# A sliding-window attention with four attention experts behind it, rewritten with other score blocks, layouts, load rules and a new list

## Chip, core, metric

The kernel runs on one core of a Trainium2 chip. The core's engines work side by side, each through its own queue in order: TensorE (PE; its weight loads are shown as PEld), VectorE (DVE), ScalarE (ACT), GpSimd (POOL) and SyncE (SP), which here only issues transfers (DMAs). Matrix products land in PSUM, which has eight banks; everything else lies in SBUF, which has 128 partitions. The metric is the device time in microseconds (us); lower is better.

## The reference, cut to what matters

Eight batches, eight heads, 576 tokens, 64 features a head. First an attention within a window of 32 tokens to both sides; its output, 512 features a token, is the input of four causal attention experts, of which each token uses two.

```python
scores = scale * np.matmul(q, k.transpose(0, 1, 3, 2))
mask = np.abs(pos[:, None] - pos[None, :]) <= 32
attn = softmax(np.where(mask, scores, -1e9))
x = np.matmul(attn, v)                  # heads side by side: [8, 576, 512]

logits = x @ w_gate                     # 4 experts
w = softmax of the 2 largest logits of a token, 0 for the others
for e in range(4):                      # one head of 64 features each
    q = x @ wq[e]; k = x @ wk[e]; v = x @ wv[e]
    a = softmax(causal(scale * (q @ k.transpose(0, 2, 1))))
    out += w[:, :, e] * (a @ v @ wo[e])
```

## The kernel before

Everything is computed in steps of a few instructions, each a small function. The string ORDER is a list of 837 steps, written out for all eight batches; the program issues them in this order, and an engine's queue holds its share of them in that order. A step's digits are its arguments (batch, head group, half, ...); what stands behind the @ names the PSUM banks. Steps of two or three batches are mixed.

*Window attention.* `lq`, `lk` load q or k of four heads (a head group) by one DMA of 576 KB: a partition gets 18 successive tokens of a head, 4608 bytes. `tq`, `tk` (both `turn`, L251) turn it on DVE, in blocks of 32 by 32, into two halves of 32 features by 576 tokens, one head on each 32 partitions; the 18 tokens of a partition are written 18 columns apart. `lv` loads V of 128 tokens at a time with eight heads side by side; `vc` (L244, L245) copies it by DMA within SBUF, so that V stands there in windows of 128 keys that start at every multiple of 64.

`sc` (L277) computes, for four heads and half of the sequence (288 queries), the scores of 64-key blocks against the queries that can see them. Blocks that start at even multiples of 64 go to PSUM partitions 0 to 63, odd ones to 64 to 127; EBLK and OBLK list them. In a block, the two feature halves of 32 are two accumulated fp32 matmuls for each of four heads, so TensorE is used as tiles of 32 rows by 64 columns. `ex` (L286) takes the exponential of two heads on ACT, `mk` (L290) multiplies by a 0/1 mask on POOL. `av` (L302) multiplies probabilities with V, 128 queries (two blocks of 64) and eight heads a step, with a 65th column of ones for the sums; step T = 4 handles the first and the last 64 queries, of which 32 each are used. `un` (L312, L313) divides by the sums on DVE and writes x with its features in an interleaved order (the feature index mod 4 outermost), to which the weight loads `lw0` to `lw2` are matched. `xt` (L322) transposes x on TensorE, `xf` (L327) copies it from PSUM in fp32 on ACT for the gate, `xb` (L337) makes a bf16 copy on POOL.

*Experts.* `ga` computes the gate's logits, `gt`, `ge`, `gm`, `gu` the two weights. `pp` and `pe` project and copy q and k of two experts, `pv` and `ve` the values, `ps` (L430) and `xe` (L436) compute causal scores and exponentials in four chunks, `se` cuts the diagonal blocks on POOL, `po` (L458) multiplies with the values, `oe` (L466) scales by gate and sum, `pt` and `ot` transpose, `py` (L482) applies the output weights, `ye` (L490) copies, `st` stores.

*Loads* are plain DMAs on SP's queue: each is issued as soon as SP is there and its buffer is free.

Of the kernel before, what the change touches and what calls it, by code (L numbers as in the profile page):

```python
# [8 lines left out]
F32 = mybir.dt.float32  # L9
# [10 lines left out]
S = 576  # L20
HS = 288
SP_ = 640

ORDER = """
    lq01 s_ones s_pads s_warm s_ident tq01 lk01 tk01 sc010@02 sc011@46 lk00 s_mask ex0100@0 mk0100 lk10 lq00
    tk00 ex0110@4 tq00 sc000@40 ex0111@6 ex0001@0 ex0000@4 lv0 sc001@60 tk10 ex0010@6 ex0101@2 lq10 tq10
    ex0011@0 lq11 vc0 lw2 lk11 lw0 lw1 lq20 lv1 tq11 mk0110 mk0111 mk0001 mk0011 mk0101 sc100@02 sc101@64
    ex1001@2 ex1010@6 mk0000 mk0010 av03@2 un03@2 av02@6 mk1010 un02@6 ex1000@0 ex1011@4 av01@0 un01@0 tk11
    lk20 av04@4 xt01@6 av00@0 xf01@6 mk1000 xb01 sc111@26 un04@4 un00@0 ex1110@2 xt02@4 cw1 xf02@4 xt00@0
    xf00@0 xb00 xb02 cw2 sc110@24 ex1101@4 ex1111@6 ex1100@2 mk1011 mk1111 lq21 ga0@0 cw0 pp001@4 gt0@0  # L30
    pp010@2 mk1100 mk1101 tq20 pe001@4 gm0 pp000@0 pp011@4 pe011@4 pv01@6 pe000@0 ge0 pe010@2 ps003@0
    ps002@2 xe003@0 mk1110 ps013@4 xe013@4 se013 ve01@6 ps000@0 vc1 mk1001 tk20 pv00@6 xe000@0 xe002@2 lk21
    ps001@0 xe001@0 ve00@6 gu0 tq21 sc200@24 ex2001@4 ex2000@2 sc201@06 av13@4 ex2011@6 ex2010@0 un13@4 lk31
    ps012@6 ps011@2 ps010@0 tk21 av14@4 un14@4 xe012@6 xe010@0 av12@6 un12@6 xe011@2 av10@0 un10@0 av11@4
    xt11@6 xf11@6 un11@4 xt12@2 se002 se003 mk2001 mk2010 po00@0 xf12@2 oe00@0 xb11 xt10@4 xb12 xf10@4
    sc211@26 sc210@40 ex2111@6 ex2110@2 ex2101@0 xb10 pp110@6 pe110@6 ex2100@4 lk30 lq30 tq30 tk30 pt00@0
    mk2011 pp111@2 pp101@6 tk31 pp100@4 pe111@2 pe101@6 lv2 lw3 cw3 pv11@1 ot00@0 ve11@1 mk2110 mk2101 se012
    mk2111 mk2100 mk2000 lq31 tq31 pe100@4 lk40 ps112@6 ps101@4 ps113@2 xe112@6 xe113@2 vc2 xe101@4 ga1@0
    sc301@26 ex3011@6 ex3010@2 gt1@0 sc300@04 tk40 mk3011 ex3001@4 ex3000@0 ps111@6 ps102@2 av22@4 un22@4
    av24@0 un24@0 xe102@2 av23@2 lq40 un23@2 av20@4 un20@4 xe111@6 mk3001 mk3010 mk3000 av21@0 sc311@26  # L40
    un21@0 tq40 sc310@04 ex3110@2 ex3111@6 ex3100@0 ex3101@4 po01@2 xt22@0 ge1 xf22@0 lk41 lq50 lq41 gm1
    oe01@2 tq41 xt21@6 xt20@4 pv10@0 ps100@2 xf20@4 xf21@6 ps103@4 mk3111 mk3101 ga2@6 ve10@0 gt2@6 lv3 lk50
    vc3 xe103@4 xe100@2 gm2 gu1 tk41 sc401@04 sc400@62 ex4010@0 mk3100 xb22 ex4001@2 ge2 ex4011@4 xb20 xb21
    pp201@0 pe201@0 pp200@2 ex4000@6 pt01@0 mk4010 ot01@0 pp210@6 pe200@2 pe210@6 ps110@0 ps200@2 xe200@2
    xe110@0 mk3110 se103 mk4001 tk50 av31@4 av34@6 un31@4 un34@6 av32@2 av33@0 un33@0 mk4000 se102 se112
    av30@6 un32@2 py00@4 py02@0 py01@2 ye02@0 ye01@2 ye00@4 pv20@0 xt31@2 tq50 un30@6 gu2 lv4 lk61 ve20@0
    st02 lq51 lk60 lk51 lq60 st01 xf31@2 sc410@46 ex4100@4 ex4101@6 se113 sc411@20 xt32@4 xf32@4 ex4111@0
    pp211@6 pe211@6 xt30@4 po11@0 mk4011 xb31 mk4101 xf30@4 mk4111 xb32 oe11@0 ex4110@2 po10@6 xb30 ps213@2
    xe213@2 ps211@4 ps210@0 ga3@2 xe210@0 xe211@4 vc4 oe10@6 gt3@2 mk4100 sc500@06 ex5000@0 ex5001@6
    sc501@42 pp301@0 tq51 tk51 ex5010@4 ex5011@2 ps203@4 xe203@4 ps202@6 xe202@6 ps212@2 ps201@4 xe212@2  # L50
    pe301@0 av41@0 un41@0 av40@6 xe201@4 un40@6 se203 mk4110 av42@2 un42@2 av44@4 av43@6 se202 mk5011 lv5
    vc5 sc510@20 ge3 ex5100@2 se212 un44@4 ex5101@0 un43@6 gm3 tk60 sc511@64 pt11@2 pv21@3 xt42@0 pt10@1
    ex5110@6 se213 mk5010 lq70 ex5111@4 ot10@1 ot11@2 pp311@6 pe311@6 ve21@3 pp300@4 tq60 gu3 pe300@4 xf42@0
    py11@6 po21@4 xt40@0 oe21@4 ye11@6 lq71 xt41@2 pp310@6 xf41@2 xf40@0 py12@4 ye12@4 pv30@2 ve30@2 pe310@6
    po20@4 oe20@4 ps311@6 ps302@0 ga4@2 xe302@0 xe311@6 gt4@2 sc601@04 ex6011@4 ex6010@0 mk5110 mk5101
    mk5111 mk5100 mk5001 xb42 sc600@62 ex6000@6 ex6001@2 av52@4 ps300@6 xe300@6 ps312@0 ps301@2 un52@4
    av53@4 xe301@2 un53@4 lv6 xb41 xb40 xe312@0 mk5000 mk6001 av50@6 av54@2 av51@0 un50@6 ps303@6 xe303@6
    un54@2 ge4 mk6000 ps313@4 ps310@2 un51@0 pp411@6 xt52@0 xe310@2 xe313@4 xt50@2 pv31@1 mk6011 xf50@2
    pe411@6 pp400@6 xt51@2 xf51@2 xf52@0 st12 lk71 lq61 tk61 ve31@1 se313 se302 pv40@4 ve40@4 se303 pe400@6
    pt20@0 pp410@2 ot20@0 tq61 po30@6 lk70 vc6 st00 lv7 pe410@2 ps413@2 xe413@2 ps412@0 ps411@4 xe412@0  # L60
    xe411@4 xb50 mk6010 py10@2 pp401@0 ye10@2 oe30@6 sc610@46 xb52 xb51 gm4 pe401@0 tk70 ex6100@4 ex6101@6
    sc611@20 ex6110@2 ex6111@0 pp501@4 pe501@4 tq70 ps403@2 se312 mk6111 mk6100 xe403@2 se403 se413 st11
    ps401@6 ps400@0 xe401@6 xe400@0 pt21@2 mk6110 mk6101 po31@4 pp500@6 pt30@3 ps402@0 oe31@4 ot30@3 ot21@2
    st10 pe500@6 xe402@0 sc701@64 tk71 sc700@02 ex7011@4 ex7010@6 ga5@4 se402 ex7001@2 ex7000@0 ps503@2
    ps410@6 xe503@2 xe410@6 gt5@4 ps501@0 ps500@2 xe501@0 xe500@2 av60@4 un60@4 av61@6 av62@0 un61@6 av63@4
    av64@6 se412 un63@4 un62@0 un64@6 py20@2 xt60@4 pv41@0 pt31@1 ve41@0 ot31@1 tq71 ye20@2 xf60@4 py22@6
    xt62@0 xf62@0 pp511@2 xt61@0 xf61@0 ye22@6 xb62 pv51@7 ve51@7 xb60 mk7010 po40@4 xb61 pe511@2 gu4 oe40@4
    pp510@0 po41@6 oe41@6 pe510@0 py21@0 ye21@0 st20 vc7 st22 st21 sc710@42 ex7100@4 ex7101@2 sc711@06 ga6@4
    mk7101 ex7111@6 ex7110@0 gt6@4 se503 mk7001 mk7100 mk7000 mk7111 ps513@6 xe513@6 ps511@2 ps502@0 xe511@2
    ps512@6 ge5 xe502@0 pp601@4 pe601@4 pp610@2 pt40@0 py30@4 pe610@2 xe512@6 py31@2 ye31@2 pt41@1 pp600@6  # L70
    pe600@6 ot40@0 pv60@2 py32@0 gm5 ot41@1 ye30@4 ye32@0 ve60@2 pv50@4 st31 ps603@2 mk7011 mk7110 se513
    ps510@0 ps601@6 xe603@2 ve50@4 av73@2 un73@2 gu5 xe510@0 av72@0 un72@0 av70@4 st32 st30 xe601@6 av74@2
    av71@6 un74@2 un71@6 un70@4 ps602@0 xe602@0 se502 po50@2 pv61@6 ve61@6 oe50@2 xt71@0 ge6 xf71@0 py42@7
    py40@4 ye40@4 xt70@0 xf70@0 ye42@7 se512 pp611@2 xt72@6 xf72@6 pe611@2 po51@4 oe51@4 ps600@2 ps612@0
    ga7@6 xe600@2 ps611@2 gt7@6 st40 xb71 xb70 se603 ps610@4 xe612@0 se602 xb72 pt51@7 py41@0 pt50@6 ot50@6
    gm7 ot51@7 xe610@4 ye41@0 xe611@2 pp701@4 pp700@0 ge7 pe700@0 py50@6 ye50@6 po60@0 gm6 pe701@4 ps703@4
    xe703@4 ps613@2 st42 st41 gu6 ps701@6 oe60@0 xe613@2 ps702@4 st50 xe702@4 ps700@2 xe700@2 xe701@6 se703
    se612 se613 pp711@0 gu7 pe711@0 py51@4 po61@2 oe61@2 py52@0 pt60@1 ye51@4 st51 pp710@6 ot60@1 ye52@0
    st52 pt61@2 pv71@3 ve71@3 ot61@2 pe710@6 ps713@6 xe713@6 ps712@0 ps711@4 xe711@4 ps710@6 xe710@6 xe712@0
    pv70@2 py61@4 py60@6 se702 se713 se712 ye61@4 ye60@6 st61 st60 ve70@2 po70@2 po71@4 oe70@2 pt70@0 oe71@4  # L80
    ot70@0 pt71@1 py62@2 ye62@2 st62 ot71@1 py71@0 ye71@0 st71 py70@2 ye70@2 st70 py72@0 ye72@0 st72
# [4 lines left out]
def kernel(  # L86
# [454 lines left out]
```

## Time and profile before

| what | us |
|---|---|
| median of 3 runs | 299.84 |
| lowest and highest run | 296.77, 302.43 |
| the profiled execution, first to last instruction (span) | 300.6 |
| PE busy with matmuls | 240.0 |
| DVE busy | 198.3 |
| ACT busy | 139.2 |
| POOL busy | 138.8 |

The profile is of one execution. Its own time is given only as the span. Busy times of engines overlap, so they don't add up; PE's ends are modelled, since its matmuls are pipelined. A fp32 matmul is recorded as two matmuls and two weight loads. "<-" behind an idle time names what ended it; "issue" stands there if nothing that the profile shows did. Lines such as L277 are lines of the kernel's file.

### The profile page before, as it was taken

The page shows a single profiled execution, that of the slowest core. Times are in us where ns is not written, and L with a number is a line of the kernel's source. Part 1 is how long each engine was busy: PE and PEld are TensorE (multiplying, and loading weights), DVE is VectorE, ACT ScalarE, POOL GpSimd, SP SyncE. Part 2 cuts the span into 40 slices and gives each one's busy share as a digit, 9 for nine tenths or more (in the row PEclk, how much of TensorE's full clock was granted, in tenths as well). Part 3 has the DMA queues.
Part 4 walks back from the last instruction along what each step waited for, and adds up shares of the span by engine and source line. Part 5 has one row for each costly group of instructions (what it writes and reads, how often), then busy time and mean ns, then how long its engine had stood idle before and what let it go on. Part 6 is the DMA issues. An engine that isn't in the chain of part 4 may idle for free.

```text
span 300.6 us, 12189 instructions
## 1 busy us (share of the span) xinstructions
PE 240.0 (80%) x5504; PEld 194.0 (65%) x5504; DVE 198.3 (66%) x351; ACT 139.2 (46%) x210; POOL 138.8 (46%) x174
## 2 busy tenths in 40 slices
PE   0745996959599589898497984999999799999973
PEld 0634974739478487777376764877777667866651
DVE  6734487866878957984819760579968527947550
ACT  1232042743356126545451454346773476278743
POOL 5358119340597245818027764053741386133210
PEclk9957598977889959999969999699999999999999
DMA  7999993199937992149957099680104413122334
GB/s 277 271 263 323 236 280 85 26 287 254 224 124 220 215 198 57 54 127 303 202 114 183 2 228 289 174 211 29 67 4 117 102 72 109 53 89 112 118 140 176
DMA packets 53396, 48.20 MB, mean 160 GB/s; under 512 B 39265, under 2 KB 40801, under 8 KB 53345
## 3 DMA queue, kind: packets, MB, share of 16 engines
q1 hardware_dynamic: 53344, 47.43, 58.1%
q8 instruction: 43, 0.70, 1.0%
q14 instruction: 9, 0.07, 0.1%
HBM read 30.42 MB, written 9.44 MB: 133 GB/s over the span
## 4 chain that ended last, share of the span: by engine, by line
PE 60%; DVE 20%; issue 13%; ACT 4%; DMA 1%; DVEq 0%; ACTq 0%
PE PS L277 15%; PE PS L302 12%; PE PS L398 8%; DVE XN L313 5%; PE PS L322 5%; PE PS L413 4%; PE PS L430 4%; PE PS L482 3%; PE PS L357 3%; DVE Tqn L251 3%; PE PS L458 3%; DVE Tkn L251 2%; DVE OE L466 2%; DVE OTT L475 1%; DMA qn<-in_q_dram 1%
## 5 line engine op out<-in xcount | busy, mean ns | idle before, releaser
L290 POOL TENSOR_TENSOR A<-A,MASKP 128x576 f32<-128x576 f32 x64 | 89.2, 1415 | 51.0 <-ACT A L286 51.0
L277 PE MATMUL PS<-Tqn,Tkn 32*64 32x128 f32 (+3 forms) x2560 | 52.5, 292 | 32.8 <-issue 18.4
L277 PEld LDWEIGHTS PS<-Tqn,Tkn 32*64 32x64 f32 x2560 | 45.2, 145 | 40.3 <-issue 25.4
L286 ACT ACTIVATE A<-PS 128x576 f32<-128x576 f32 x64 | 38.6, 649 | 58.4 <-PE PS L277 54.0
L436 ACT ACTIVATE ATE<-PS 128x1024 bf16<-128x1024 f32 (+1 forms) x64 | 50.6, 837 | 28.2 <-PE PS L430 26.4
L302 PE MATMUL PS<-V,A 128*64 128x65 f32 x1280 | 47.2, 241 | 5.4 <-issue 5.1
L302 PEld LDWEIGHTS PS<-V,A 128*64 128x64 f32 x1280 | 45.2, 155 | 8.8 <-issue 7.1
L442 POOL TENSOR_SCALAR_AFFINE_SELECT ATE<-ATE 128x384 bf16<-128x384 bf16 (+2 forms) x64 | 25.9, 435 | 48.4 <-ACT ATE L436 47.0
L313 DVE TENSOR_TENSOR XN<-PS,RC 128x512 f32<-128x512 f32 x40 | 42.6, 1065 | 1.6 <-DVE RC L312 0.2
L251 DVE STREAM_TRANSPOSE Tkn<-kn 128x576 f32<-128x576 f32 x32 | 37.1, 1241 | 8.3 <-PE PS L277 8.3
L251 DVE STREAM_TRANSPOSE Tqn<-qn 128x576 f32<-128x576 f32 x32 | 37.0, 1240 | 1.6 <-DMA qn<-in_q_dram 1.6
L337 POOL CAST XTB<-XTF 128x1024 bf16<-128x1024 f32 x16 | 16.5, 1039 | 41.9 <-ACT XTF L327 41.7
L327 ACT COPY XTF<-PS 128x1024 f32<-128x1024 f32 x16 | 16.0, 1014 | 25.1 <-PE PS L322 24.2
L312 DVE RECIPROCAL RC<-PS 128x8 f32<-128x8 f32 x40 | 7.8, 195 | 26.5 <-PE PS L302 25.6
L322 PE MATMUL PS<-ident,XN 128*128 128x128 f32 x160 | 22.6, 289 | 1.5 <-DVE XN L313 0.7
L430 PE MATMUL PS<-QKE 64*128 64x64 bf16 (+4 forms) x192 | 18.2, 300 | 6.0 <-issue 3.6
L482 PE MATMUL PS<-WO,OTT 128*128 128x512 bf16 x80 | 20.4, 379 | 2.1 <-DVE OE L466 0.9
L406 DVE CAST QKE<-PS 128x576 bf16<-128x576 f32 x16 | 12.1, 755 | 15.1 <-PE PS L398 11.9
L398 PE MATMUL PS<-XTB,WK 128*128 128x288 bf16 x128 | 19.4, 297 | 3.1 <-issue 2.7
L322 PEld LDWEIGHTS PS<-ident,XN 128*128 128x128 f32 x160 | 19.2, 150 | 3.5 <-DVE XN L313 1.1
L413 PE MATMUL PS<-WV,XTB 128*128 128x256 bf16 x160 | 20.1, 273 | 1.7 <-ACT Y L492 1.6
L398 PE MATMUL PS<-XTB,WQ 128*128 128x288 bf16 x128 | 20.7, 313 | 0.0
(64 smaller groups left out, 242.4 us busy)
## 6 DMA issues: line engine op xcount, KB each, us to landing
qn<-in_q_dram SPq DMA_DIRECT2D x16, 576.0 KB, 6.8
kn<-in_k_dram SPq DMA_DIRECT2D x16, 576.0 KB, 6.6
V<-in_v_dram SPq DMA_DIRECT2D x32, 256.0 KB, 6.6
out_dram<-Y SPq DMA_DIRECT2D x16, 512.0 KB, 3.1
V<-V SPq DMA_DIRECT2D x8, 528.0 KB, 8.4
V<-V SPq DMA_DIRECT2D x8, 396.0 KB, 9.5
V<-in_v_dram SPq DMA_DIRECT2D x8, 128.0 KB, 4.7
out_dram<-Y SPq DMA_DIRECT2D x8, 128.0 KB, 2.6
```

What stands on the lines that cost most here:

```text
L251: nc.vector.transpose(T[:, dh, :].rearrange("q (p o) -> q o p", o=18), n_[:, :, 32 * dh:32 * dh + 32])
L277: nc.tensor.matmul(sl[hh // 2][64 * par:64 * par + 64, hh % 2, lo - c0:hi - c0], KT[r, dh, k0:k0 + 64], QT[r, dh, lo:hi], start=(dh == 0), ...
L286: nc.scalar.activation(a_part(b, g, half, p), two(b0)[:, :, 0:HS], EXP, scale=scale_att)
L290: nc.gpsimd.tensor_tensor(out=ap, in0=ap, in1=MASK[:, None, HS * half:HS * half + HS].to_broadcast([128, 2, HS]), op=MULT)
L302: nc.tensor.matmul(u[64 * i:64 * i + 64, h // 4, 65 * (h % 4):65 * (h % 4) + 65], A[:, h % 4, c:c + 64], V[:, slot, h, 0:65], start=True, ...
L313: nc.vector.tensor_tensor(out=xdst(T).rearrange("p (t g h s) -> p g h s t", t=4, g=2, s=16), in0=u[:, :, :, 0:64].rearrange("p g h (s t) - ...
L322: nc.tensor.transpose(o[:, 128 * dt:128 * dt + 128], XN[w][:, i, 128 * dt:128 * dt + 128], ident)
L398: nc.tensor.matmul(o[:, half, 0:HS], WQK[j][n][:, dt, :], W[:, dt, HS * half:HS * half + HS], start=(dt == 0), stop=(dt == NDT - 1))
L413: nc.tensor.matmul(o, W[:, dt, 128 * t:128 * t + 128], WV[:, dt, :], start=(dt == 0), stop=(dt == NDT - 1))
L430: nc.tensor.matmul(o[:, eo, at:at + hi - lo], Q[r, 1, 128 * kt:128 * kt + 128], Q[r, 0, lo:hi], start=True, stop=True, skip_group_check=True)
L436: nc.scalar.activation(A[:, :, 512 * c:512 * c + w], two(b0)[:, :, 0:w], EXP, scale=scale_moe)
L482: nc.tensor.matmul(o, OTT[b % 2][:, j, 128 * t:128 * t + 128], WO[:, j, :], start=(j == 0), stop=(j == 1))
```

## The change

The kernel is rewritten in place; what is computed stays. The parts:

- *Scores.* Of the blocks of half a sequence, one is now of 128 keys (tiles of 32 rows by 128 columns) and three are of 64. Where a narrower block shares a region with the wide one, it is computed after it and overwrites it.

```diff
-    EBLK = [[(0, 0, 96), (1, 96, 224), (2, 224, 288)], [(2, 288, 352), (3, 352, 480), (4, 480, 576)]]
-    OBLK = [[(0, 0, 160), (1, 160, 288)], [(2, 288, 416), (3, 416, 576)]]
+    BLK = [[(0, 1, 128, 96, 288), (0, 0, 64, 0, 96), (1, 0, 64, 0, 160), (0, 2, 64, 224, 288)],
+           [(0, 2, 128, 288, 416), (0, 3, 64, 352, 480), (1, 3, 64, 416, 576), (0, 4, 64, 480, 576)]]
...
+        for par, m, n, lo, hi in BLK[half]:
+            k0 = 128 * m + 64 * par
             for dh in range(2):
+                for hh in range(4):
+                    r = slice(32 * hh, 32 * hh + 32)
+                    mm(PS[64 * par:64 * par + n, bank[hh], lo - c0:hi - c0], K[dh][r, k0:k0 + n], Q[dh][r, lo:hi],
+                       start=(dh == 0), stop=(dh == 1), skip_group_check=True)
```

- *q and k.* A head's tokens are laid out as pairs, pair p of every 64 on partition p: a tile comes by four DMAs (one a head, 32 partitions), in rows of 512 bytes, and the turned tokens of a partition are written two columns apart. Only the first batch's tiles are loaded and turned in two parts, and part of them from ACT's queue (":t"). The modes "e" and "f" are not used by the list.

```diff
+            for h in range(4):
+                load(t[32 * h:32 * h + 32, 2 * m0:2 * m1, :].rearrange("p (m o) d -> p m (o d)", o=2),
+                     src[b, 4 * g + h].rearrange("(m p o) d -> p m (o d)", p=32, o=2)[:, m0:m1, :], queue)
...
+                nc.vector.transpose(T[:, 64 * m0:64 * m1].rearrange("q (m p o) -> q m o p", p=32, o=2),
+                                    n_[:, 2 * m0:2 * m1, 32 * dh:32 * dh + 32].rearrange("p (m o) d -> p m o d", o=2))
```

- *Loads tied to TensorE.* A load depends on the last TensorE instruction that stands ahead of it in the list. V comes in five separate steps a batch.

```diff
+    def load(o, i, q_=nc.sync):
+        r = q_.dma_start(o, i)
+        if last_pe[0] is not None:
+            tc.add_manual_dep(r.ins, last_pe[0].ins.name,
+                              mybir.DependencyInfo(mybir.DependencyClass.Sync, mybir.DependencyReason.DATA),
+                              reason="load follows its place in the list")
```

- *V's second copy* is made by an engine instead of by DMA, two copies a batch: 12 on POOL, 2 on DVE, 2 on ACT. V rows have 65 elements instead of 66.

```diff
-        nc.sync.dma_start(pairs[64:128, :, 1, :], pairs[64:128, :, 0, :])
-        nc.sync.dma_start(pairs[0:64, 0:3, 1, :], pairs[0:64, 1:4, 0, :])
+        if par:
+            copy(c, pairs[64:128, :, 1], pairs[64:128, :, 0])
+        else:
+            copy(c, pairs[0:64, 0:3, 1], pairs[0:64, 1:4, 0])
```

- *Features in natural order, ends as one tile.* `un` writes x in the order of heads and features; the weights are loaded to match, in rows of 256 bytes. The first and last 32 queries of eight heads are computed as one tile of 128 partitions by 256 features: `av` with T = 4 uses TensorE in columns of 32, `un` handles half the elements, `xt` needs two transposes instead of four.

```diff
-            out=xdst(T).rearrange("p (t g h s) -> p g h s t", t=4, g=2, s=16),
-            in0=u[:, :, :, 0:64].rearrange("p g h (s t) -> p g h s t", t=4),
-            in1=rc[:, :, :, None, None].to_broadcast([128, 2, 4, 16, 4]), op=MULT)
+            nc.vector.tensor_tensor(out=XN[T // 2][:, T % 2, :].rearrange("p (g h d) -> p g h d", g=2, h=4),
+                                    in0=u[:, :, :, 0:64], in1=rc[:, :, :, None].to_broadcast([128, 2, 4, 64]), op=MULT)
...
+            for hh in range(4):
+                for g in range(2):
+                    for e, (slot, c0) in enumerate(((0, 0), (7, 544))):
+                        r = 64 * g + 32 * e
+                        mm(PS[r:r + 32, b0, 65 * hh:65 * hh + 65], prob(b, 4 * g + hh, c0, 32), V[:, slot, 4 * g + hh, :],
+                           start=True, stop=True, skip_group_check=True, tile_position=(0, r))
```

- *The last 64 tokens of the experts.* `pv` and `py` compute them as two halves of TensorE's columns, `pt` transposes 64 columns, and the store is two DMAs.
- *Which engine.* A step names the engine of its copy or mask (":v" DVE, ":a" ACT, ":g" POOL). Of 64 masks 23 go to DVE, the rest stay on POOL. The copies from PSUM (`xf`, `pe`, `ve`, `ot`, `ye`) and the bf16 copies `xb` are shared out in the same way; before, each kind had one engine.
- *Buffers.* PSUM is one tile of eight banks, of which a step takes any neighbouring pair; masked scores are held in four smaller tiles a head group; the expert scores of a chunk lie together, and POOL cuts the diagonals in 80 instructions instead of 64.
- *The list* is another one of 917 steps, in another order and on other banks. Its start (`lq100` is q of batch 1, head group 0, whole; the third digit is the part of the tile; `sc010@02` is batch 0, group 1, first half, from banks 0 and 2):

```
    s_mask s_pads lq100 lk011:t tk011:t lk001:t tk001:t lq011 lq001 tq011 lq002 lk012:t lk002:t lq012 s_ones
    sc010@02 lv02 lk100 lv01 lv03 s_warm tq001 sc000@46 ex0101@2 ex0001@6 mk0001:g ex0000@4 lv00 s_ident mk0101:g
...
```

In numbers of instructions: TensorE goes from 5504 to 5024 matmuls (as recorded, two for a fp32 product that is no transpose) with as many weight loads, scores from 2560 to 2048; SP issues 206 transfers instead of 118, ACT 16 instead of none.

More of the change, by code (lines that the diff above doesn't have):

```diff
@@ L412, in pv @@
+    def pv(c, b, part, b0):
+        W = XTB[b % 2]
+        if part == 0:
+            for t in range(4):
+                for dt in range(NDT):
+                    mm(PS[:, b0 + t // 2, 256 * (t % 2):256 * (t % 2) + 256], W[:, dt, 128 * t:128 * t + 128], WV[:, dt, :],
+                       start=(dt == 0), stop=(dt == NDT - 1))
+        else:
             for dt in range(NDT):
[L413 to L414 removed]
```

552 lines of the change are left out of this document (295 added, 257 removed).

## The prediction

> **What bounds the kernel now.** I read the page's totals first, then the time by 40 us windows, PE's waits, PE's timeline around the longest of them, and the DMA queues.
>
> ```profile
> span 300.6 us, 12189 instructions
> ...
> PE 240.0 (80%) x5504; PEld 194.0 (65%) x5504; DVE 198.3 (66%) x351; ACT 139.2 (46%) x210; POOL 138.8 (46%) x174
> ```
>
> ```profile
> PE 60%; DVE 20%; issue 13%; ACT 4%; DMA 1%; DVEq 0%; ACTq 0%
> PE PS L277 15%; PE PS L302 12%; PE PS L398 8%; DVE XN L313 5%; PE PS L322 5%; PE PS L413 4%; PE PS L430 4%; PE PS L482 3%; PE PS L357 3%; DVE Tqn L251 3%; PE PS L458 3%; DVE Tkn L251 2%; DVE OE L466 2%; DVE OTT L475 1%; DMA qn<-in_q_dram 1%
> ```
>
> ```profile
> 0.00:40.00 40.00, 22.68 (x672) 19.90 (x675) 23.21 (x40) 9.76 (x15) 18.82 (x25) 0.79 0.97 277
> 120.00:160.00 40.00, 33.41 (x823) 27.18 (x822) 27.16 (x44) 19.16 (x29) 18.20 (x25) 0.91 0.65 160
> 240.00:300.00 60.00, 50.97 (x805) 37.12 (x790) 31.80 (x75) 36.59 (x52) 21.73 (x35) 0.99 0.30 109
> ```
>
> Totals, the chain of work that ended last, and three windows: length, busy time of PE, PEld, DVE, ACT and POOL, then the granted clock, the DMA share and GB/s. PE is the fullest engine and has most of the chain. But it is busy 85% of the last 60 us, at a clock of 0.99 and a DMA share of 0.30, and only 57% of the first 40, at 0.79 and 0.97. So PE is held up where transfers are dense. What holds it:
>
> ```profile
> PE PS L277 <- issue: 18.4, 10, 4.1
> ...
> PE PS L302 <- issue: 5.1, 3, 4.2
> ...
> PE PS L430 <- issue: 3.6, 1, 3.6
> PE PS L398 <- issue: 2.7, 1, 2.7
> ```
>
> ```profile
> q1 hardware_dynamic: 53344, 47.43, 58.1%
> q8 instruction: 43, 0.70, 1.0%
> ```
>
> ```profile
> 115.65 2.26 PE L277 MATMUL PS<-Tqn,Tkn 32*64 32x64 f32 x131
> 118.39 0.67 PE L277 MATMUL PS<-Tqn,Tkn 32*64 32x128 f32 x29 [0.48 <-issue]
> ...
> 144.66 1.72 PE L277 MATMUL PS<-Tqn,Tkn 32*64 32x96 f32 x102
> 150.50 1.86 PE L277 MATMUL PS<-Tqn,Tkn 32*64 32x64 f32 x58 [4.12 <-issue]
> ...
> 238.96 2.60 PE L277 MATMUL PS<-Tqn,Tkn 32*64 32x96 f32 x160
> ```
>
> PE's waits (total, times, longest), the DMA queues (packets, MB, share) and PE's timeline. "issue" means that nothing in the profile released PE. These four add up to 29.8 us. PE has 5504 matmuls and as many weight loads, 11008 instructions, and queue 8 brought instructions in 43 packets: 256 instructions a packet. The idle in front of 118.39 comes after 131 matmuls with their loads, about one such piece. I read these waits as PE running out of fetched instructions. Two score steps, 320 instructions, take 2.60 us undisturbed, so a piece of scores is used up in 2.1 us, while the next was there no sooner than 2.7 us after the last (115.65 to 118.39, where PE waited), and where transfers are dense it came 4 us late. A second cost stands behind each long wait:
>
> ```profile
> 188.00:193.50 5.50, 5.37 (x77) 0.50 0.91 229
> sum 27.40, PE 27.22; mean PE 5.44
> ```
>
> The last of five windows, each behind a wait of 3 us or more, and their sum: PE is busy throughout, at a granted clock of 0.50 in each. The same work at full clock would need 13.6 us less.
>
> **The change, part by part.** The sum is made against the span, 300.6 us; the runs' median, 299.84, is the same within their spread, so I convert one to one.
>
> ```profile
> L302 PE MATMUL PS<-V,A 128*64 128x65 f32 x1280 | 47.2, 241 | 5.4 <-issue 5.1 <-ACT A L286 0.2
> ...
> L277 PE MATMUL PS<-Tqn,Tkn 32*64 32x160 f32 x512 | 29.1, 330 | 1.6 <-issue 1.6
> L322 PE MATMUL PS<-ident,XN 128*128 128x128 f32 x160 | 22.6, 289 | 1.5 <-DVE XN L313 0.7 <-ACT Y L492 0.7
> ...
> L413 PE MATMUL PS<-WV,XTB 128*128 128x256 bf16 x160 | 20.1, 273 | 1.7 <-ACT Y L492 1.6
> ...
> L277 PE MATMUL PS<-Tqn,Tkn 32*64 32x64 f32 x512 | 17.7, 251 | 5.4 <-issue 4.1 <-ACT A L286 0.6 <-DVE VE L419 0.3
> ```
>
> *Scores.* A score step goes from 40 matmuls, each two passes, to 32. A pass costs (330-251)/96 = 0.82 ns a column of queries. Before, the even and the odd key blocks fill two halves of the array side by side, 288 columns each: 288 x 2 feature halves x 2 passes x 0.82 = 0.94 us, measured 1.30, so 0.36 goes to filling and weights. After, the 128-key block has the whole array to itself (192 columns in one half of the sequence, 128 in the other), then the 64-key blocks share it (160 beside 160; 224 beside 160): 352 columns, 1.15 us. With the 0.36, and 0.05 for one more change of tile shape (taken small: the shape changes at every step already), 1.56: 0.26 more a step, over 32 steps **+8.3 us**. Bounds: -8.3 (a fifth fewer instructions, were they the limit) to +17 (below).
>
> *Instruction fetch.* The scores go from 5120 to 4096 instructions, 20 pieces to 16, and a piece now lasts two steps, 3.1 us instead of 2.1. If a fetch takes 4.3 us from the last, as a middle value, pieces of scores alone would lack 20 x 2.2 = 44 us before and 16 x 1.2 = 19 after; scaled to the 29.8 measured (pieces are mixed with slower steps), 13 us remain. If the fetch is quicker, 3.5 us, the same ratio leaves 16 x 0.4 x 29.8/44 = 4. It should be quicker: the V<-V copies on queue 1 go (8 x 924 KB = 7.4 of 47.4 MB), and a load no longer starts as soon as its buffer is free, but waits for the last PE instruction ahead of it in the list, so that they come a quarter or half a megabyte at a time. I take 8 left: **-22 us**, bounds 0 and -30. With the waits goes the half clock, in proportion: 13.6 x 22/30 = **-10 us**, bounds 0 and -13.6.
>
> *The ends as one tile, and smaller last tiles.* Transposes of x: 144 instead of 160, at 22.6/160 = 0.14 us, -2.3. The fifth probability-times-V tile (a fifth of 47.2 us = 9.4) puts four 32-column jobs side by side instead of two: at best half, I take -3. The value products of the last 64 tokens (a fifth of 20.1) fill two halves at once: half, -2; the output products, cut alike, are taken to give as much. Together **-9 us**, bounds -12 and -3.
>
> ```profile
> L313 DVE TENSOR_TENSOR XN<-PS,RC 128x512 f32<-128x512 f32 x40 | 42.6, 1065 | 1.6 <-DVE RC L312 0.2
> L251 DVE STREAM_TRANSPOSE Tkn<-kn 128x576 f32<-128x576 f32 x32 | 37.1, 1241 | 8.3 <-PE PS L277 8.3
> L251 DVE STREAM_TRANSPOSE Tqn<-qn 128x576 f32<-128x576 f32 x32 | 37.0, 1240 | 1.6 <-DMA qn<-in_q_dram 1.6
> L466 DVE TENSOR_TENSOR OE<-PS,RG 128x640 bf16<-128x640 f32 x16 | 13.2, 824 | 0.5
> ```
>
> ```profile
> L290 POOL TENSOR_TENSOR A<-A,MASKP 128x576 f32<-128x576 f32 x64 | 89.2, 1415 | 51.0 <-ACT A L286 51.0
> ```
>
> *VectorE.* L313 writes with a stride and takes 2.1 ns an element; L466, also from PSUM but writing in sequence, takes 1.29. In natural feature order 512 elements should take 660 ns; 32 of these and eight halves are 24 us instead of 42.6. The q,k transposes wrote 18 elements apart and now write two apart. Bounds: 1240 ns as now, and 576 x 1.29 = 740; I take 800, nearer the second because neighbours now lie together: 64 x 0.44 = 28 us less. [...] New on DVE: 23 of the 64 masks (at L466's rate 0.74, as on POOL 1.42; I take 0.76, the element count being what DVE's rows follow, so 17 us), and about 10 us net of copies. DVE falls from 198 to about 180 us. ACT takes more copies, about 157; POOL gives 23 masks away (-33) and gets 12 V copies of 1536 or 2048 elements (some 23 us at 1 ns an element), about 127 with the finer causal cuts. None reaches PE. What counts is the chain: XN and T there are 10% of the span, 30 us, and lose a third: -10; masks and copies queued ahead of them on the in-order DVE give some back, +2. **-8 us**, bounds -15 and +8.
>
> ```profile
> qn<-in_q_dram SPq DMA_DIRECT2D x16, 576.0 KB, 6.8
> ```
>
> ```profile
> 134.72 0.43 SPq L225 DMA_DIRECT2D qn<-in_q_dram  x1
> ```
>
> *Loads.* A q or k tile is four DMAs instead of one, rows of 512 bytes instead of 4608 (the issue list: KB, median us to landing; then the timeline of SP): SP has 206 DMAs instead of 118, at 0.43 us unhindered 89 us, well inside the span. Behind a load that waits for PE stand SP's later loads and stores; DVE's transposes and POOL's V copies wait for it. In the list most loads stand 5 to 12 us of PE work ahead of their user; four issues and a landing need 1.3 + 6.8 at most, less for quarter tiles. That cover can be thin: **+2 us**, bounds 0 and +10. The start: SP issues batch 1's first q tile (4 x 0.43) ahead of the q that the first score needs, while k comes on ACT's queue and in parts: **+1**, bounds -1 and +4.
>
> *At nothing:* PSUM as one tile with any pair of banks, masked scores in four smaller tiles, V rows of 65 elements: they change what may be waited for, not the work.
>
> Sum: 300.6 + 8.3 - 22 - 10 - 9 - 8 + 2 + 1 = 263. I keep 262, since with DVE's steps shorter the small waits of PE on XN, OE and T that the chain does not show shrink as well.
>
> **The rivals.**
> *A. PE nearly without gaps.* 3 us of fetch left, all of the clock back, scores limited by instructions (0): 300.6 - 27 - 13.6 - 9 - 11 + 1 = 241. For it: the last 60 us already run so. Against it: the two halves of the array were full. Chance 0.17.
> *B. Score blocks in strict order.* A block then starts only when the last pass of the block ahead has started, and the odd 64-key block no longer runs beside both even ones. By passes of 0.82 ns a column the first half of the sequence takes 0.63 + 0.24 + 0.39 + 0.21 = 1.47 us and 0.11 more for filling and 0.2 for the shape: 1.8 a step, +17 instead of +8.3: 271. [...] Against it: x160 in 2.60 us is close to the two halves independent, but even and odd blocks alternate there, so it decides little, and no other row here does. Chance 0.16.
> *C. The loads are not spread.* If the tie does nothing (loads that were late anyway; the list puts 14 load steps within its first 256 PE instructions), and 512-byte packets keep the queue as full, waits and clock stay: 300.6 + 8.3 - 9 - 8 + 3 = 295. Chance 0.09.
> *D. Slower: fetch becomes the bound.* 36,864 q,k packets of 512 bytes where 4096 of 4608 were stand in the same queues. Should every fetch take as long as the worst now (144.66 to 150.50 and more, about 7 us), 10,048 instructions are 39 pieces x 7.2 = 281, plus 8 at the start, 4 at the end, and 17 of waits on other engines: 310. It makes the kernel slower from 7.1 us a piece on; against it, 2.7 us sufficed at 115.65 and the V<-V traffic is gone. Chance 0.08.
>
> **The numbers.** Forecast 262, chance 0.50, by itself 248 to 278. 2% is what a measurement here can tell from no change (the runs lie within 1% of their median): faster is under 294. Faster: 0.50 + 0.17 + 0.16 and a third of C, 0.86; same: most of C and a little of D, 0.07; slower: 0.07. The range runs from 237 to 292: it leaves out D (0.08), two thirds of C (0.06) and the lower third of A (0.06).
>
> **What would show it.** Right: PE's "issue" waits under 12 us; clock above 0.95; the scaling of XN near 660 ns, transposes near 800; a score step of 64 passes near 1.5 us; no V<-V on queue 1. Wrong: issue waits near 30 (C), a PE that stops at most 256-instruction borders (D), score steps of 1.8 (B), or PE waiting for T or V from a late load.

## The result, and the profile after

The changed kernel takes 264.56 us (median of 4 runs, 264.01 to 265.06), the kernel before 299.17 beside it (4 runs, 296.77 to 302.43): a ratio of 0.888, with a 95% interval of 0.882 to 0.893. Ratios here and below compare only the faster executions of both kernels, so they differ a little from the quotient of the medians. The forecast was 262. The profiled execution has a span of 262.5 us against 300.6.

The totals, the chain and the DMA queues of the page after:

```profile
span 262.5 us, 11479 instructions
...
PE 228.9 (87%) x5013; PEld 183.2 (70%) x5024; DVE 193.2 (74%) x400; ACT 147.0 (56%) x221; POOL 127.2 (48%) x165
...
q1 hardware_dynamic: 86752, 38.69, 64.4%
...
q8 instruction: 39, 0.64, 1.1%
...
PE 64%; DVE 16%; DMA 9%; issue 3%; ACT 3%; SPq 2%; POOL 1%; ACTq 0%; DVEq 0%
```

PE is busy 87% of the span instead of 80%, and "issue" has 3% of the chain instead of 13%. PE's waits after (total, times, longest):

```profile
PE PS L179 <- DVE Tqn L298: 11.6, 1, 11.6
PE PS L179 <- ACT A L336: 3.5, 4, 1.3
PE PS L179 <- DVE XN L368: 2.4, 1, 2.4
...
PE PS L179 <- issue: 0.2, 1, 0.2
```

The waits for instructions are gone. That they were waits for instructions was the prediction's reading; the trace of the kernel before bears it out. It has 16 idle times of PE that it puts down to issue, 30.3 us. Counting what PE's queue had started by then (matmuls, weight loads and the few other instructions that the trace holds), each of the 15 over 0.4 us ends 193 to 195 instructions behind a multiple of 256, so all of them lie whole pieces of 256 apart. And each of the 16 ends 1.1 to 1.5 us behind the end of a packet of queue 8.

The longest wait left is the start, 11.6 us; it was 8.05 (first row of the next fence). PE's waits sum to 26.9 us (issue 0.2, DVE 21.1, ACT 5.0, POOL 0.6) against 55.4 before (issue 30.3, DVE 20.3, ACT 4.8). Two rows of PE's timeline before (start, length), the second for the score steps below:

```profile
8.05 0.84 PE L277 MATMUL PS<-Tqn,Tkn 32*64 32x96 f32 x16 [8.05 <-DVE Tkn L251]
...
241.49 0.47 PE L357 MATMUL PS<-XTF,WG 128*32 128x160 f32 x7
```

The stretches in which the granted clock was half, first of before, then of after (length, busy time of PE, clock, DMA share, GB/s; the first of nine rows and their sum, then the first of two and their sum; the last row of either is the end of the kernel, without work of PE):

```profile
16.10:26.30 10.20, 5.88 (x204) 0.50 1.04 289
...
sum 52.40, PE 40.30; mean PE 4.48
```

```profile
21.00:31.20 10.20, 8.22 (x180) 0.50 0.97 199
...
sum 12.80, PE 8.22; mean PE 4.11
```

PE worked 40.3 us at half clock before and 8.2 after. Taken as twice the time at full clock, as the prediction took it, 20.1 us of PE's busy time were the clock's before and 4.1 are after. That is an upper estimate: after, a score step takes 2.9 us at half clock (5.75 for the two from 25.92) and 1.70 at full. The rows of the clock don't show all of it: the first score steps after,

```profile
11.64 6.54 PE L179 MATMUL PS<-Tqn,Tkn 32*128 32x192 f32 x132 [11.64 <-DVE Tqn L298]
```

take 3.0 us each as well, in windows whose clock is given as 1.00. The trace has no entry for the clock ahead of 12.7 us before and of 17.6 after. Estimated as half of PE's busy time up to there, another 2.2 us were lost before and 3.0 after. Two score steps, undisturbed, on PE's timeline after:

```profile
117.06 3.47 PE L179 MATMUL PS<-Tqn,Tkn 32*128 32x192 f32 x128
120.46 1.04 PE L179 MATMUL PS<-WO,OTT 128*128 128x512 bf16 x3
```

From start to start of what follows, 3.40 us, 1.70 a step. Before, the pair that starts at 238.96 is followed at 241.49: 1.265 a step. So 32 steps cost 32 x 0.435 = 13.9 us more, an estimate from these two pairs. With this the two spans can be told apart term by term:

| term, us | before | after | difference | predicted |
|---|---|---|---|---|
| PE waits on "issue" | 30.3 | 0.2 | -30.1 | -22 |
| PE busy: what half clock adds | 20.1 | 4.1 | -16.0 | -10 |
| PE busy: 32 score steps | | | +13.9 | +8.3 |
| PE busy: what is left of 240.0 - 228.9 = 11.1 | | | -9.0 | -9 (ends) |
| PE waits on other engines, start among them | 25.1 | 26.7 | +1.6 | -5 (VectorE -8, loads +2, start +1) |
| gaps too short for the list | 5.2 | 6.7 | +1.5 | |
| span | 300.6 | 262.5 | -38.1 | -38 |

The last term of PE's busy time is a remainder, not a measurement of the ends alone; what was lost at the start ahead of the clock's first entry lies in it too. And the table tells one execution of each kernel. The kernel before varies: its mean granted clock is 0.913 in the profiled execution and 0.918 to 0.945 in 21 others, so a few us of its waits and of its half clock belong to this execution.

### The profile page after: what moved, and what is told of

The parts are those of the page before. It is cut to its first block, busy times and chain, and to the rows that moved or that the text cites. A ratio compares the mean times of both kernels' runs of the same rounds, so it can differ in the third digit from the quotient of the medians.

```text
span 262.5 us, 11479 instructions
## 1 busy us (share of the span) xinstructions
PE 228.9 (87%) x5013; PEld 183.2 (70%) x5024; DVE 193.2 (74%) x400; ACT 147.0 (56%) x221; POOL 127.2 (48%) x165
## 3 DMA queue, kind: packets, MB, share of 16 engines
q10 hardware_dynamic: 2560, 1.18, 2.4%
## 4 chain that ended last, share of the span: by engine, by line
PE 64%; DVE 16%; DMA 9%; issue 3%; ACT 3%; SPq 2%; POOL 1%; ACTq 0%; DVEq 0%
PE PS L179 57%; PE PS L182 7%; DVE A L340 5%; DMA qn<-in_q_dram 4%; DMA kn<-in_k_dram 4%; SPq L185 2%; ACT A L336 2%; DVE Tkn L298 1%; DVE RG L545 1%; DVE OE L546 1%; DMA out_dram<-Y 1%; DVE XN L368 1%; POOL V L173 1%; DVE Tqn L298 1%; DVE VE L173 1%
## 5 line engine op out<-in xcount | busy, mean ns | idle before, releaser
L179 PE MATMUL PS<-Tqn,Tkn 32*64 32x96 f32 (+5 forms) x2048 | 63.6, 307 | 16.9 <-DVE Tqn L298 11.6
L340 POOL TENSOR_TENSOR A<-A,MASKP 128x576 f32<-128x576 f32 x41 | 59.2, 1458 | 33.1 <-ACT A L336 32.5
L179 PEld LDWEIGHTS PS<-Tqn,Tkn 32*64 32x64 f32 (+1 forms) x2048 | 51.9, 158 | 29.4 <-DVE Tqn L298 12.0
L506 ACT ACTIVATE ATE<-PS 128x1024 bf16<-128x1024 f32 x48 | 47.4, 1023 | 8.4 <-PE PS L179 6.8
L511 POOL TENSOR_SCALAR_AFFINE_SELECT ATE<-ATE 128x256 bf16<-128x256 bf16 (+1 forms) x80 | 31.4, 413 | 39.6 <-ACT ATE L506 24.2
L179 PE MATMUL PS<-V,A 128*64 128x65 f32 (+1 forms) x1280 | 39.6, 222 | 3.8 <-DVE XN L368 2.4
L179 PEld LDWEIGHTS PS<-V,A 128*64 128x64 f32 (+1 forms) x1280 | 36.1, 132 | 7.5 <-DVE XN L368 2.9
L173 POOL COPY V<-V 64x2048 f32<-64x2048 f32 (+1 forms) x12 | 21.8, 1820 | 27.3 <-DMA V<-in_v_dram 21.9
L298 DVE STREAM_TRANSPOSE Tkn<-kn 128x576 f32<-128x576 f32 (+2 forms) x36 | 23.2, 686 | 8.4 <-DMA kn<-in_k_dram 7.3
L298 DVE STREAM_TRANSPOSE Tqn<-qn 128x576 f32<-128x576 f32 (+2 forms) x36 | 23.2, 686 | 7.6 <-DMA qn<-in_q_dram 6.6
L340 DVE TENSOR_TENSOR A<-A,MASKP 128x576 f32<-128x576 f32 x23 | 25.3, 1109 | 3.0 <-ACT A L336 3.0
L368 DVE TENSOR_TENSOR XN<-PS,RC 128x512 f32<-128x512 f32 x32 | 22.1, 691 | 1.1
L179 PE MATMUL PS<-WO,OTT 128*128 128x512 bf16 (+1 forms) x85 | 18.2, 341 | 1.4 <-ACT OTT L171 0.7
```

The lines of the kernel that those rows point to most:

```text
L173: eng(c).tensor_copy(o, i)
L179: last_pe[0] = nc.tensor.matmul(*a, **kw)
L298: nc.vector.transpose(T[:, 64 * m0:64 * m1].rearrange("q (m p o) -> q m o p", p=32, o=2), n_[:, 2 * m0:2 * m1, 32 * dh:32 * dh + 32].rearr ...
L340: eng(c).tensor_tensor(out=ap, in0=ap, in1=MASK[:, None, HS * half:HS * half + HS].to_broadcast([128, 2, HS]), op=MULT)
L368: nc.vector.tensor_tensor(out=XN[T // 2][:, T % 2, :].rearrange("p (g h d) -> p g h d", g=2, h=4), in0=u[:, :, :, 0:64], in1=rc[:, :, :, N ...
L506: nc.scalar.activation(chunk(A, ch), two(b0), EXP, scale=scale_moe)
```

## The experiments

Five theories are named by letters in the expectations. T: tying loads to TensorE took the fetch waits away. N: fewer score instructions did. Q: the V<-V transfers were what instruction packets waited behind. P: q,k rows of 4608 bytes were. L: where loads stand in the list counts, not their form. The kernel before took 302.4, 301.6 and 300.7 us (medians of 7) beside the three groups of runs; ratios are to the runs of the same group. For two kernels single runs lie up to 2% apart from the rest and no ratio is given; their runs stand instead.

### In the changed kernel, one part put back

**a_no_tie**, loads issued as soon as SP and the buffer are there:

```diff
-        if last_pe[0] is not None:
+        if False:
```

> The changed kernel with the tie of loads to TensorE taken out; every load is issued when SP is there and its buffer is free. Theory T (the tie took PE's fetch waits away, by spreading the loads): PE's waits put down to issue rise from 0.2 to 15-25 us, some half clock returns, 280-295 us. Theory N (fewer score instructions) and theory Q (no V<-V traffic): waits stay under 3 us, 262-267 us.

271.41 us (268.69 to 273.58), ratio 0.911 (0.892 to 0.931). PE's waits on issue:

```profile
PE PS L179 <- issue: 3.9, 4, 2.1
```

The tie is worth 3.7 us of fetch waits, where T expected 15 to 25, and some 7 us of time. T names a real but small part.

**a_blocks64**, the blocks of before, 80 passes a step:

```diff
-    BLK = [[(0, 1, 128, 96, 288), (0, 0, 64, 0, 96), (1, 0, 64, 0, 160), (0, 2, 64, 224, 288)],
+    BLK = [[[(0, 0, 64, 0, 96), (1, 0, 64, 0, 160)], [(0, 1, 64, 96, 224), (1, 1, 64, 160, 288)], [(0, 2, 64, 224, 288)]],
```

> The changed kernel with the score blocks of before: 64-key blocks only, even and odd ones in turn, 80 passes a step instead of 64. All theories: a step takes about 1.27 us instead of 1.70, which is 14 us over 32 steps. Theory N: a piece of 256 score instructions lasts 2.0 us again, less than the 2.7 of the quickest fetch, so issue waits of 10-20 us come back and the time is 260-270. Theories T and Q: waits stay under 5 us, 249-254 us.

269.27 us (264.57 to 269.84). PE is busy 221.3 us instead of 228.9. That is 7.6 us less, where the shorter steps alone should bring 13.9: by the estimate used above half clock takes 2 us more here (the clock's first entry is at 31.0 us), and score steps with a wait inside take 1.6 to 2.1 us beside it, the others 1.4 to 1.5. And PE waits:

```profile
PE PS L179 <- issue: 10.0, 11, 2.3
```

All of PE's waits are 40.6 us instead of 26.9, 9.8 of the difference on issue, which is more than the shorter steps save. N's forecasts, 10 to 20 us of issue waits and 260 to 270 us, both hold.

**a_v_by_dma**, V's second copy as two transfers on SP's queue, as before:

```diff
-            copy(c, pairs[64:128, :, 1], pairs[64:128, :, 0])
+            nc.sync.dma_start(pairs[64:128, :, 1], pairs[64:128, :, 0])
```

> The changed kernel with V's second copy made by the two DMAs of before instead of POOL, DVE and ACT. Theory Q: 7.4 MB more on queue 1 slow the fetches, issue waits of 6-15 us, 270-282 us. Theories T and N: waits under 3 us; POOL is rid of 22 us, but the copy lands 5 us or more after its issue and stands in SP's queue ahead of loads, so 263-268 us.

311.04 us (309.71 to 312.44), ratio 1.049 (1.029 to 1.069): slower than before. Its first row of PE's waits:

```profile
PE PS L179 <- DMA V<-V: 40.7, 5, 12.3
```

Issue has only 0.9 us here, so in this kernel Q fails, and no theory expected 311 us. PE waits for the copy itself. One of the five waits on the timeline (start, length):

```profile
100.91 1.80 SPq L185 DMA_DIRECT2D kn<-in_k_dram  x4
102.76 0.62 SPq L315 DMA_DIRECT2D V<-V  x1
103.42 0.62 SPq L317 DMA_DIRECT2D V<-V  x1
108.88 3.40 PE L179 MATMUL PS<-V,A 128*64 128x65 f32 x61 [7.74 <-DMA V<-V]
```

V's last load had landed at 98.0; the copy goes out behind four loads of k on the same queue and needs 6 us more (5.8 to 6.0 in the median from issue to landing), where GpSimd takes 1.8 us for a copy in the changed kernel. With this list the way of copying matters: by an engine the copy is in time, by DMA it is not.

**a_old3**, these three put back at once:

> The changed kernel with all three undone: no tie, 64-key blocks, V copied by DMA. If these three together are what took the waits away: issue waits 20-30 us, several stretches at half clock, 280-292 us (264.5 - 14 for the shorter score steps + 25 + 10). If the new list alone did it: waits under 5 us, 250-256 us.

292.01 us (288.18 to 292.98), ratio 0.979 (0.956 to 1.003); PE's waits:

```profile
PE PS L179 <- issue: 10.5, 11, 2.9
PE PS L179 <- DMA V<-in_v_dram: 10.4, 1, 10.4
PE PS L179 <- DMA V<-V: 9.3, 2, 5.8
```

All issue waits together are 11.7 us, where 20 to 30 were expected. The three together cost less than the V copies alone. Loads that are not tied come earlier, which would fit; no run has that pair alone. What is put back doesn't add up.

**a_turn18**, the 56 whole-tile transposes write 18 columns apart; **a_rows18**, the same with q and k of batches 1 to 7 in one DMA a tile and rows of 4608 bytes (the first two lines are a_rows18's, which takes up a way to load and turn that the kernel has but doesn't use; the others a_turn18's):

```diff
-        if c in ("e", "f"):
+        if part == 0:
...
+                if part == 0:
+                    nc.vector.transpose(T[:, :].rearrange("q (p o) -> q o p", o=18), n_[:, :, 32 * dh:32 * dh + 32])
+                    continue
```

> The changed kernel, the 56 whole-tile q,k transposes writing 18 columns apart as before, loads as they are (so tokens of later batches are permuted). Each transpose 1240 ns instead of 753, DVE +27 us busy. If the transposes lie on the path as the chain of before had them: +4 to +6, 268-271 us. If DVE, at 83% of the span then, becomes the bound: 278-290. If they are hidden: 264-266. Issue waits under 2 us.

> The changed kernel, q and k of batches 1 to 7 loaded as before by one DMA a tile in rows of 4608 bytes and turned 18 apart (right result). It differs from the kernel with only the transposes undone by the form of the load alone. Theory P (it is the 4608-byte rows in the queue that instruction packets wait behind): PE's issue waits 5-20 us, the packets start up to 3-4 us after PE enters a piece, 8-20 us slower than that kernel. Theory L (the place of the loads in the list matters, not their form): issue waits under 2 us, within 2 us of that kernel or faster, since 28 DMAs replace 112.

281.36 us (275.74 to 282.09) and 281.39 (279.63 to 283.76; ratio 0.933, 0.925 to 0.941). Three of a_turn18's four runs lie at 280.7 to 282.1, its profiled one among them. So the form of the loads makes no difference beyond the scatter of the runs with this list, and issue waits are 0.2 and 1.9 us: P falls here. The turns alone cost 17 us by the medians (11 by a_turn18's fastest run), more than the prediction gave to all of VectorE. **a_strided** adds the old writing order of XN:

> The changed kernel with both of VectorE's writing orders as before: the whole-tile transposes 18 columns apart (tokens come out in another order) and XN with its features interleaved (they no longer match the weights), so what is computed is not the reference; the amount of work is. VectorE then works 193 + 24 + 12 = 229 us. If VectorE sets the pace of the middle of the kernel (it is busy 37 to 38 of 40 us there with the turns alone changed), the 12 us of the scaling cost 5 to 12 us beyond the turns alone: ratio to before 0.95 to 0.98, and VectorE is busy over 37 of 40 us in two or three windows. Rival (only the terms on the chain count, as in the prediction): 0.935 to 0.95.

287.53 us (283.41 to 287.93), ratio 0.958 (0.921 to 0.996), 23 us above the changed kernel and 6 above a_turn18, as its first forecast has it. Windows of a_strided (length, busy time of PE, PEld, DVE, ACT, POOL, clock, DMA share, GB/s):

```profile
80.00:120.00 40.00, 35.40 (x847) 28.75 (x847) 38.45 (x65) 20.87 (x32) 20.18 (x18) 1.00 0.67 158
120.00:160.00 40.00, 34.13 (x841) 26.88 (x837) 37.55 (x56) 18.10 (x31) 23.75 (x27) 1.00 0.51 131
```

VectorE is busy 38 of 40 us there, more than PE, and sets the pace: PE's waits on DVE are 36.4 us against 21.1, +15.3, and PE works 21.8 us at half clock against 8.2, +6.8. The sum, 22.1, is the 23.0 between the spans, 285.5 and 262.5. In a_turn18 the same two terms are 9.8 and 6.8, of 16.5.

**a_start**, batch 1's first q tile behind batch 0's loads in the list:

```diff
-    s_mask s_pads lq100 lk011:t tk011:t ... lq002 lk012:t lk002:t lq012 s_ones
+    s_mask s_pads lk011:t tk011:t ... lq002 lk012:t lk002:t lq012 lq100 s_ones
```

> The changed kernel with one step of the list moved: the load of batch 1's first q tile from the front to behind batch 0's loads. SP's issues to the first q are four fewer, about 0.5 us each here: first matmul at 9.5-10.2 us instead of 11.6. If the start is on the path: 262-263 us. If what follows waits anyway (the batch 1 tile comes later, ACT's exponentials bound the first steps): no change.

264.91 us (264.17 to 265.97), against 264.56 (264.01 to 265.06) for the changed kernel: no gain. (The ratio, 0.878, 0.873 to 0.883, is lower because the kernel before took longer beside it.) The first score began 1 us earlier:

```profile
10.69 5.56 PE L179 MATMUL PS<-Tqn,Tkn 32*128 32x192 f32 x123 [10.69 <-DVE Tqn L298]
```

That was given back later. The tile that was moved accounts for 1.0 of the 3.6 us by which the changed kernel starts later; the rest stays open.

### In the kernel before, one part added

**b_mixed**, the new score blocks; **b_pairs**, 512-byte rows in four DMAs a tile and turns two apart; **b_v_pool**, V's second copy on GpSimd. List, untied loads and the rest stay. Their core lines:

```diff
+    BLK = [[(0, 1, 128, 96, 288), (0, 0, 64, 0, 96), (1, 0, 64, 0, 160), (0, 2, 64, 224, 288)],
...
+        for h in range(4):
+            nc.sync.dma_start(t[32 * h:32 * h + 32, :, :].rearrange("p (m o) d -> p m (o d)", o=2),
+                              src[b, 4 * g + h].rearrange("(m p o) d -> p m (o d)", p=32, o=2))
...
+        nc.gpsimd.tensor_copy(pairs[64:128, :, 1], pairs[64:128, :, 0])
+        nc.gpsimd.tensor_copy(pairs[0:64, 0:3, 1], pairs[0:64, 1:4, 0])
```

> The kernel before, with only the score blocks of the changed kernel (one block of 128 keys and three of 64 in half a sequence, 64 passes instead of 80); list, loads, V's copy and VectorE's steps stay. N (fewer score instructions end the fetch waits): 'issue' waits of PE fall from 30 us to 10 to 18, packets on queue 8 from 43 to 39, and the time to 0.95 to 0.98 of before, since the longer steps (32 times 0.43 = 14 us of PE) lie where PE waited for instructions anyway. Rival (the waits come from the transfers, not from the number of instructions): issue waits stay at 22 us or more, the longer steps are added, ratio 1.00 to 1.04.

> The kernel before with one part of the change: q and k in rows of 512 bytes, four DMAs a tile, turned two columns apart. Theory P: PE's issue waits fall from 30 to 8-18 us, with less half clock, and the transposes save DVE 28 us: ratio 0.89-0.94 (268-283 us). Theory L: issue waits stay at 22-30, only the transposes gain: ratio 0.96-0.99.

> The kernel before, with V's second copy made by GpSimd instead of by DMA; all else stays. Q (the V<-V transfers are what instruction packets and loads wait behind): PE's waits on V<-V vanish, issue waits fall from 30 to 15 to 24 us, ratio 0.96 to 0.985. Rival (the copies were hidden, and GpSimd with 139 us of its own gets some 28 more, ahead of masks): issue waits 26 to 30, PE waits on A or V by POOL of 3 to 8 us appear, ratio 0.99 to 1.02.

PE's longest waits on issue, b_mixed, then b_pairs, then b_v_pool:

```profile
PE PS L272 <- issue: 6.6, 3, 3.1
PE PS L297 <- issue: 6.1, 5, 1.8
```

```profile
PE PS L278 <- issue: 11.8, 5, 2.9
PE PS L303 <- issue: 2.8, 4, 1.5
```

```profile
PE PS L277 <- issue: 8.6, 6, 3.4
PE PS L302 <- issue: 4.4, 3, 2.5
```

| kernel | time, us | ratio (95%) | PE waits: issue | DVE |
|---|---|---|---|---|
| before | 299.17 | | 30.3 | 20.3 |
| b_mixed | 292.37 | 0.979 (0.959 to 1.000) | 13.0 | 22.8 |
| b_pairs | 296.84 | 0.983 (0.977 to 0.989) | 17.0 | 28.4 |
| b_v_pool | 303.61 | 1.005 (0.965 to 1.045) | 18.2 | 31.2 |
| b_all3 | 300.16 | 0.994 (0.964 to 1.024) | 0.8 | 40.1 |

In the one profiled execution of each, every part by itself has 12 to 17 us less of fetch waits than the kernel before, as N, Q and P expected; how far these waits vary between executions was not measured. In b_pairs the rows, the number of DMAs and the turns changed together, so which of them it was stays open, and its time lies where L put it, not P. Only b_mixed and b_pairs turn some of it into time, about 2%, and b_mixed's interval ends at 1.000. In b_v_pool PE waits 10.9 us more on DVE, and the time is that of before, as its rival had it.

**b_all3** has the three at once:

> The kernel before with three parts of the change at once: the score blocks of b_mixed, the rows and turns of b_pairs, V's second copy on GpSimd. The list of steps, untied loads, the scaling of XN and the ends stay as before. If these parts carry the gain whatever the list: issue waits under 8 us and ratio 0.92 to 0.95, so that the list with all the rest is worth 0.04 to 0.06 more. Rival (the new list, which shares out copies and masks and sets its loads apart, carries most of it): issue waits 8 to 18 us, new waits on transfers or on POOL, ratio 0.96 to 1.00.

Issue waits are gone, 0.8 us, as the first theory wanted, and the time is that of before, as the rival wanted. Three rows of PE's waits show most of where it went:

```profile
PE PS L273 <- DVE Tkn L252: 9.8, 1, 9.8
PE PS L468 <- DVE QKE L402: 7.8, 1, 7.8
PE PS L273 <- DVE Tqn L252: 6.2, 2, 3.2
```

Against before, issue waits fall by 29.5 us and half clock by 7.7 ((40.3 - 24.8)/2); waits on DVE rise by 19.8, on POOL by 2.5, and the score steps are 13.9 longer by the estimate above. Together that is -1.0 us; the two spans, 295.3 and 300.6, differ by 5.3. The first and third row are the start, where the first q and k tiles come in four loads each: 16.0 us, against 11.9 for the same rows before. The second row on the timeline (start, length):

```profile
111.01 2.02 POOL L333 CAST XTB<-XTF 128x1024 bf16<-128x1024 f32 x2
...
112.11 7.11 DVE L377 SCALAR_TENSOR_TENSOR LZ<-GE,LT 128x20 f32<-128x20 f32 x1
...
113.00 2.75 POOL L286 TENSOR_TENSOR A<-A,MASKP 128x576 f32<-128x576 f32 x2
...
115.97 2.74 POOL L286 TENSOR_TENSOR A<-A,MASKP 128x576 f32<-128x576 f32 x2
118.67 1.34 POOL L438 TENSOR_SCALAR_AFFINE_SELECT ATE<-ATE 128x384 bf16<-128x384 bf16 x3
...
121.97 0.72 DVE L402 CAST QKE<-PS 128x576 bf16<-128x576 f32 x1
122.74 0.69 PE L468 MATMUL PS<-ident_bf,OE 128*128 128x128 bf16 x5 [7.79 <-DVE QKE L402]
```

A step of 20 elements a partition takes 7.11 us on DVE; the shortest of its eight kind takes 0.18 and their median is 0.83. POOL works without a pause all that time; the section on the hardware comes back to it. Everything behind it on the in-order DVE waits, and PE with it.

## Why the prediction was right, and where its steps were off

The forecast of 262 us stands 2.6 us from the median, and its main step holds: PE ran out of instructions, and the changed kernel does not. Of the views that were named for it, all but one came out: issue waits under 12 us (0.2), a clock above 0.95 (0.975), no V<-V on queue 1, and the two of VectorE below; a score step takes 1.70 us and not 1.5. For VectorE's steps, groups by shape of the kernel after:

```profile
L340 DVE TENSOR_TENSOR A<-A,MASKP 128x576 f32<-128x576 f32 x23 | 25.3, 1109 | 3.0 <-ACT A L336 3.0
L368 DVE TENSOR_TENSOR XN<-PS,RC 128x512 f32<-128x512 f32 x32 | 22.1, 691 | 1.1
L298 DVE STREAM_TRANSPOSE Tkn<-kn 128x576 f32<-128x576 f32 x28 | 20.0, 754 | 3.8 <-DMA kn<-in_k_dram 2.7 <-PE PS L179 1.1
```

XN takes 691 ns (660 expected) and a whole transpose 754 (800 expected). That the sum came out within 3 us is luck in part: fetch and half clock gave 14 us more than forecast, and scores, waits on other engines and short gaps took 14 back.

- *Instruction fetch, -22: measured -30, at its bound.* Of the three reasons given, fewer score instructions is shown from both sides (10 us of waits come back without them, b_mixed has 17 less with them). No V<-V goes with 12 us less in the kernel before (b_v_pool), but the copies bring none back in the changed one (a_v_by_dma). The third, loads that wait for PE, is worth little (3.7 us of waits). That the smaller rows might hurt (rival D) was wrong: where they came in with four DMAs a tile and the new turns (b_pairs), the waits fell.
- *Half clock, -10: measured -16.* The prediction counted five stretches behind waits of 3 us or more, 27.2 us of work; there are eight with work, 40.3 us, and the longest, 16.10 to 26.30, was not among the five.
- *Scores, +8.3: measured +13.9.* The step of the working that failed is "0.05 for one more change of tile shape". In the step at 117.06 the passes of the 128-key block follow each other by 0.16 us, as 192 columns by 0.82 ns say; but 0.27 us pass after the first, and 0.27 before the first 64-key pass. Both are 0.11 more than a pass, and the step behind it (128 columns) has 0.10 and 0.11 as well. In the pair at 238.96 of the kernel before, either step has such a delay once, of 0.05. So the new blocks add some 0.16 a step, not 0.05: over 32 steps 3.5 of the 5.6 us that were missed. The rest stays open.
- *Rival B's time, 1.8 us a step, came nearer, by another cause.* Its strict order, an assumption, is refuted. The program issues all 16 passes of the even 96-column block ahead of the odd 160-column one. Groups by shape in the 0.1 us from 117.90 on:

```profile
L179 PE MATMUL PS<-Tqn,Tkn 32*64 32x160 f32 x4 | 0.4, 345 | 0.0
...
L179 PE MATMUL PS<-Tqn,Tkn 32*64 32x96 f32 x4 | 0.3, 292 | 0.0
```

  Four passes of each have begun; the even block's other twelve start from 118.05 to 118.24. So they run side by side. The trace of before could have told it: from 239.34 us four passes of the next even block (128 columns) start ahead of the last four of the odd block (160 columns, from 239.44), which stand earlier in the program.
- *VectorE, -8: the term as the prediction put it is not there.* PE's waits on DVE are 21.1 us, 20.3 before; without the start (11.6, 8.05) they fall by 2.7. The chain of the kernel before showed what these steps cost in the old list. In the new one they carry 23 masks and more copies as well, and with the old writing orders it is 23 us slower (a_strided). So the faster steps are worth far more than -8 to the new list. That most of it is spent on the work moved there would fit; no run shows it.
- *The start, +1: measured +3.6*, inside the bound of +4. *The ends, -9*: the remainder of PE's busy time agrees, no run shows them alone.

What no run settles is which of the other changes bring b_all3's 300 us down to 264.6: the list, the tie, XN's order, the shared-out copies and masks, the ends. They were not tried one by one in the old list. What is shown is that removing the fetch waits is not enough by itself, and that the parts work together: blocks, rows and turns, and V's copy in the old list gain 0.6% (b_all3); the changed kernel without the blocks, V's copy and the tie gains 2.1% (a_old3); neither is clear of no gain. Everything together gains 11%.

## What to carry to other kernels

In the kernel before, PE outran the fetch of its own program, by the reading above of its 30.3 us of idle time that nothing releases. The signs were that the 15 waits over 0.4 us lay whole multiples of 256 instructions apart, and that each of the 16 ended 1.1 to 1.5 us behind the end of a packet of the instruction queue. Fewer, longer instructions took more than half of it away in b_mixed (13.0 us left), but a wait taken away need not become time: in b_v_pool 12.1 us less on issue came with 10.9 us more on DVE, and the ratio is 1.005. Half clock was a term of its own, at most 20.1 us before and 4.1 after; count every stretch of it. And the parts of such a change depend on the list that they stand in: single parts put back here cost 5 to 46 us and single parts added to the old list gained 8 to -3, so neither sum gives the worth of the parts.

## What the runs showed of the hardware that was not expected

*Masks on DVE that began beside a GpSimd instruction ended behind it.* On the timeline of the kernel after, a mask on POOL and two on DVE:

```profile
98.61 1.41 POOL L340 TENSOR_TENSOR A<-A,MASKP 128x576 f32<-128x576 f32 x1
98.64 2.00 DVE L340 TENSOR_TENSOR A<-A,MASKP 128x576 f32<-128x576 f32 x1
101.28 0.75 DVE L340 TENSOR_TENSOR A<-A,MASKP 128x576 f32<-128x576 f32 x1
```

The one that began beside POOL's took 2.00 us and ended 0.62 us after it; the second, beside which POOL was idle until 101.86, took 0.75. POOL's was not slowed: its 1.41 us are the median of the 41 masks there. All 23 masks on DVE agree: the nine that began while a POOL instruction had 0.2 us or more to go took 0.85 to 2.48 us, and each ended 0.61 to 0.62 us behind that instruction; the other 14 took 0.71 to 0.76. XN, which reads PSUM, took 690 to 692 ns in the eight cases of 32 that began in the same way, with a mean of 691 over all 32. The 7.11 us in b_all3 reach over seven POOL instructions in a row and end 0.04 us behind the seventh, so in this one case the DVE instruction did not end behind the first of them. Such cases are why masks given to DVE measure 1109 ns in the mean where 750 is the median, and in b_all3 PE waited 7.79 us behind one.

*Some 0.1 us more pass behind the first pass of a 128-key block, and again ahead of the first 64-key pass.* From pass to pass it is 0.27 instead of 0.16 us with 192 columns and 0.21 to 0.22 instead of 0.11 with 128, twice a step, in 22 of the 25 steps from 40.45 us on in the kernel after. Over 32 steps that is some 7 us, by estimate from these times. That the change of shape is the reason is a reading of these times; no run has the shapes apart.
